# Second-layer output weights prepared while the input half runs, parked in DRAM and read back

## The chip, the core and the metric

The kernel runs on one core of a Trainium2 chip: TensorE (PE in the profile) for matmuls, VectorE (DVE), ScalarE (ACT), GpSimd (POOL), and SyncE (SP), which here only issues DMA transfers. Each engine works through its own queue in order. The metric is device time in microseconds, the median of several runs.

## The reference

Local plus downsampled attention gives x of 2304 tokens by 512. Two feed-forward layers follow, in float32:

```python
h = x @ w_in;  g = where(h > 0, h, exp(min(h, 0)) - 1);  x = g @ w_out        # first layer
h = x @ w2_in; r = maximum(h, 0); g = s * (r * r) + b;   out = g @ w2_out     # second layer
```

w_in and w2_in are 512 x 2048, w_out and w2_out are 2048 x 512. The weights come as float64, so they have to be turned into float32 on the core before use.

## The kernel before

**Two halves of the second layer.** The w2_in half (h and g of all tokens) has its first product at 542.3 us, among the last ones of the first layer, and its last at 742 us; the w2_out half follows. The stretch in which the weight tiles pass from one to the other is called the exchange here. A float32 product is made of three passes: each operand is split into a rounded part (hi) and the remainder (lo), and hi x hi, lo x hi and hi x lo are added in PSUM.

**Seven products instead of eight.** Tokens are taken as five groups: four groups of two 256-token blocks and one single block (group 3). For a pair of blocks, 2 x 2 blocks are multiplied with seven products (numbers 1 to 7, in the order ROW for w2_in and COL for w2_out) of sums and differences of half-matrices. So each weight pair p (eight pairs, 256 of the 2048 columns each) needs two tiles: the values (wb) and four half-matrix sums (wa), both as hi and lo.

**Making a weight pair**, `halves(kind, p, due)` (L1238): one load of 1 MB of float64 into a `raw` tile; Prelu on ACT (L1256), a shift (L1258) and a combine (L1260) on DVE, which give float32 values; four sums of 256 columns on DVE (L1277); then a hi copy on ACT and a lo remainder on DVE or POOL for the values (L1279, L1281) and for the sums (L1283, L1284). kind 0 is w2_in, kind 1 is w2_out. hi and lo of w2_out go to the same 16 SBUF tiles that hold w2_in's, so they can be written only when the last group has used those.

**Units and quads.** `unit` (L1382) makes seven products of twelve 256-column matmuls for two pairs (four units a group), DVE adds the PSUM banks into h tiles (`total`, L1432), ACT applies Relu (L1442), Square (L1370) and the affine step (L1376), and SP stores the tile to DRAM as `gd` (L1443). `quad` (L1456) loads four g tiles (`gb`, L1469), makes sums of them on DVE (L1496 to L1502), splits each of seven operands into an F tile (ACT L1478, DVE or POOL L1479) and runs one half, 24 matmuls on four pairs, per operand. Two quads make a group.

**Places.** SBUF outside the weights is an arena: `ar.place` (L46) gives a tag n tiles at an offset of a ground, with a phase. A place can be used once all places of earlier phases under it are through. The nine `st` places hold h tiles, seven `X` the split inputs, three `F` the split g operands, `raw1` one raw w2_out tile, `cv` five converted pairs, `St` two sets of sums.

**What sets the order.** The code describes operations with a due time. `Plan.emit` (L147) then lays them out with a price for each, always taking the soonest or the most urgent, and writes each engine's queue in that order; the waits between engines follow from the data. `MM` is the price of one 256-column matmul, `GBS` that of a byte of DMA, which `slow` multiplies. Where the plan sees PE idle, `fill` (L132) calls `keep_warm` (L1542), which puts matmuls on a zero tile `wz` into PE's queue (L1548): their number is fixed when the program is built.

## Time and profile before

| | |
|---|---|
| median of 3 runs | 942.58 us (939.83 to 944.01) |
| profiled execution | 943.77 us |
| its span, first to last instruction | 942.0 us |
| PE busy | 931.9 us, 99% |
| DVE, ACT, POOL busy | 701.4, 556.8, 398.3 us |
| mean granted TensorE clock | 0.989 |
| moved by DMA | 126.1 MB, 134 GB/s on average |

Busy time counts the zero-tile matmuls of L1548 as PE work, so PE's share alone doesn't tell how much of it is products. For a wait, the engine's own timeline and the chain of work that ended last are to be read together: the chain says which engine's work the end hung on in each stretch. Starts in a timeline are exact; a duration of matmuls that follow each other overlaps the next one, so the time of a run is the distance between starts.

### The profile page before, as it was taken

How to read it: one execution, taken by the hardware profiler on the slowest of the kernel's cores; microseconds unless marked ns; L12 is line 12 of the kernel's file. 1: busy time of each engine (PE TensorE's matmuls, PEld its weight loads, DVE VectorE, ACT ScalarE, POOL GpSimd, SP SyncE). 2: the span in 40 equal slices, each digit the busy share in tenths (PEclk: the TensorE clock that was granted, in tenths of full speed). 3: DMA queues.
4: the chain of work that ended last, by engine and by line, in shares of the span. 5: the costliest groups of instructions: out<-in, count | busy, mean ns of one | idle time of the engine just before them, and what ended most of it. 6: DMA issues, size and time to landing. Idle time of an engine off the chain costs nothing. (4 is left out here: it accounts for less than half of the span.)

```text
span 942.0 us, 21568 instructions
## 1 busy us (share of the span) xinstructions
PE 931.9 (99%) x8577; PEld 882.9 (94%) x8577; DVE 701.4 (74%) x1087; ACT 556.8 (59%) x1207; POOL 398.3 (42%) x356
## 2 busy tenths in 40 slices
PE   8999999999999999999999999999999999999998
PEld 4879999999999999999999999999999679999998
DVE  5467768888887889888716688777549988786875
ACT  5488766564554545444656678887978734334332
POOL 4567657797887778776456742000001100000000
PEclk9599999999999999999999999999999999999999
DMA  9739776545442425334112255636545353343511
GB/s 192 192 120 233 201 183 164 142 135 116 111 129 69 132 60 146 97 101 119 62 44 92 88 183 190 192 131 215 174 130 168 118 183 125 102 157 116 167 36 42
DMA packets 118917, 126.11 MB, mean 134 GB/s; under 512 B 50464, under 2 KB 93472, under 8 KB 118816
## 3 DMA queue, kind: packets, MB, share of 16 engines
q1 hardware_dynamic: 117024, 124.29, 46.1%
q8 instruction: 67, 1.10, 0.5%
q10 hardware_dynamic: 1792, 0.44, 0.2%
q14 instruction: 34, 0.28, 0.1%
HBM read 92.73 MB, written 31.98 MB: 132 GB/s over the span
## 5 line engine op out<-in xcount | busy, mean ns | idle before, releaser
L1034 PE MATMUL acc<-split,w 128*128 128x256 f32 x1728 | 234.6, 285 | 0.0
L1034 PEld LDWEIGHTS acc<-split,w 128*128 128x128 f32 x1728 | 216.4, 188 | 2.9 <-issue 1.9
L988 PE MATMUL h<-split,w 128*128 128x256 f32 x1488 | 204.9, 286 | 0.9 <-DVE work L1012 0.7
L988 PEld LDWEIGHTS h<-split,w 128*128 128x128 f32 x1488 | 188.6, 190 | 3.7 <-DVE work L1012 1.3
L413 POOL TENSOR_TENSOR split<-work,split 128x256 fp32r<-128x256 f32 (+2 forms) x156 | 141.9, 917 | 92.6 <-ACT split L405 80.9
L1487 PE MATMUL acc<-w,attn 128*128 128x256 f32 x864 | 106.2, 281 | 0.0
L405 ACT ACTIVATE split<-work 128x256 fp32r<-128x256 f32 (+2 forms) x162 | 66.5, 423 | 64.5 <-PE acc L1034 30.9
L1487 PEld LDWEIGHTS acc<-w,attn 128*128 128x128 f32 x864 | 104.1, 189 | 0.0
L1012 DVE SCALAR_TENSOR_TENSOR work<-work,h 128x256 f32<-128x256 f32 x124 | 50.5, 414 | 67.5 <-ACT work L1010 67.1
L1422 PE MATMUL acc<-attn,w 128*128 128x256 f32 x768 | 99.7, 282 | 0.0
L1422 PEld LDWEIGHTS acc<-attn,w 128*128 128x128 f32 x768 | 95.3, 188 | 0.0
L1008 ACT ACTIVATE work<-h 128x256 f32<-128x256 f32 x124 | 47.1, 380 | 75.9 <-PE h L988 49.7
L1478 ACT ACTIVATE attn<-work 128x1024 fp32r<-128x1024 f32 x35 | 37.2, 1062 | 64.6 <-DVE work L1502 22.7
L1479 POOL TENSOR_TENSOR attn<-split,attn 128x1024 fp32r<-128x1024 f32 x2 | 5.4, 2682 | 158.4 <-PE at L1422 155.5
L413 POOL TENSOR_TENSOR work<-work 128x896 f32<-128x896 f32 (+1 forms) x41 | 68.2, 1672 | 5.9 <-DVE work L930 5.4
L930 DVE TENSOR_REDUCE work<-work 128x128 f32<-128x896 f32 x36 | 63.5, 1788 | 4.8 <-POOL work L413 4.8
L1010 ACT ACTIVATE work<-work 128x256 f32<-128x256 f32 x144 | 60.0, 416 | 3.9
L1376 ACT ACTIVATE split<-split,sb 128x512 f32<-128x512 f32 x62 | 48.6, 808 | 12.0 <-DVE split L1373 11.2
L1487 PE MATMUL h<-w,attn 128*128 128x256 f32 x432 | 54.6, 281 | 0.7 <-DVE attn L1479 0.7
L1487 PEld LDWEIGHTS h<-w,attn 128*128 128x128 f32 x432 | 52.5, 189 | 1.0 <-DVE attn L1479 0.9
L1479 DVE TENSOR_TENSOR attn<-work,attn 128x1024 fp32r<-128x1024 f32 x35 | 42.4, 1221 | 12.8 <-ACT attn L1478 12.5
L1422 PE MATMUL h<-attn,w 128*128 128x256 f32 x384 | 51.4, 282 | 0.0
(194 smaller groups left out, 1651.6 us busy)
## 6 DMA issues: line engine op xcount, KB each, us to landing
gd<-split SPq DMA_DIRECT2D x57, 256.0 KB
split<-gd SPq DMA_DIRECT2D x28, 512.0 KB
work<-in_moe_w_in_dram SPq DMA_DIRECT2D x16, 512.0 KB
work<-in_moe_w_out_dram SPq DMA_DIRECT2D x16, 512.0 KB
work<-in_moe_w_in_dram SPq DMA_DIRECT2D x8, 1024.0 KB
work<-in_moe_w_out_dram SPq DMA_DIRECT2D x8, 1024.0 KB
work<-in_k_dram SPq DMA_DIRECT2D x17, 320.0 KB
work<-in_v_dram SPq DMA_DIRECT2D x17, 320.0 KB
```

The costliest lines, as they stand in the source:

```text
L405: a = (0.11 + n / 1200, lambda: nc.scalar.activation(out=out(), in_=src(), func=ACTF.Copy, scale=scale))
L413: f = lambda e: lambda: e.tensor_tensor(out=out(), in0=in0(), in1=in1(), op=alu)
L930: op("dve", 0.07 + 14 * D / 546, lambda: nc.vector.tensor_reduce(out=vo()[:, WD + j * D:WD + (j + 2) * D].rearrange("p (j d) -> p j d", j= ...
L988: nc.tensor.matmul(ps(), lhsT=w()[:, wpart, 0, c * 128:(c + 1) * 128], rhs=x.at(xpart)[:, c, :], start=first and i == 0, stop=last and i = ...
L1008: op("act", ta + 0.07, lambda: nc.scalar.activation(out=e(), in_=ps(), func=ACTF.Relu, scale=-1.0), r=[ps], w=[r1], u=[e], due=due)
L1010: op("act", ta, lambda: nc.scalar.activation(out=e(), in_=e(), func=ACTF.Exp, scale=-1.0), r=[r1], w=[r2], u=[e], due=due)
L1012: op("dve", td, lambda: nc.vector.scalar_tensor_tensor(out=e(), in0=e(), scalar=-1.0, in1=ps(), op0=ALU.add, op1=ALU.max), r=[r2, ps], w=[ ...
L1034: nc.tensor.matmul(acc()[:, c * N:(c + 1) * N], lhsT=wo[:, cc * 128:(cc + 1) * 128], rhs=g(), start=first and c == 0, stop=end and c == 1)
L1376: [lambda: nc.scalar.activation(out=h(), in_=h(), func=ACTF.Identity, scale=sb2[:, 0:1], bias=sb2[:, 1:2]), lambda: nc.vector.tensor_scala ...
L1422: nc.tensor.matmul(ps[:, q * 256:(q + 1) * 256], lhsT=factor(0, w[2 * u + q], i, wi, c), rhs=x[i]()[:, xi].rearrange("p (c t) -> p c t", c ...
L1479: on(lambda e: e.tensor_tensor(out=f()[:, 1], in0=src(), in1=f()[:, 0].bitcast(F32), op=ALU.subtract), 1024, ("dve", "pool"), r=[*r, hi], ...
L1487: nc.tensor.matmul(m[i]()[:, c * 256:(c + 1) * 256], lhsT=f()[:, xi, o:o + 128], rhs=factor(1, w[pair], i, wi, 0), start=qd == 0 and p == ...
```

## The change

`halves` is split up. `weights` loads and converts a pair and makes its sums. For w2_in, `halves` then splits them into hi and lo as before. For w2_out, `ahead` runs `weights` for all eight pairs while the w2_in half is on, from the second group on by its due times, twelve us apart, and stores the float32 values (`wb`) and the sums (`wa`) to DRAM, 512 KB each. At the exchange `kept_halves` loads them back into `cv` tiles and only makes hi (ACT) and lo (DVE).

Places change with it: w2_out's raw tiles use the two `raw` places, the converted values get three `cw` places, the first four g tiles lie where `raw` was and need not wait for h tiles, `sq` moves to the ground `split`, and `cv` has four places.

Numbers of the plan change too: a matmul is priced 0.1185 us instead of 0.1085, the second layer's large transfers at 0.85 of the byte price, x2d loads are due 11 us earlier, and the seven products of a unit run in the order 1, 2, 6, 7, 5, 4, 3.

```diff
     RAW, EV, R_, WU = 0, 16384, 24576, 26624
+    ar.place("cw", 1, 4096, "work", 0, 1, EV)
+    ar.place("cw", 2, 4096, "work", 0, 2, WU + 4096)
     ar.place("X", 7, 4096, "attn", 1, 1)
...
     ar.place("st", 1, 2048, "work", 0, 1, R_)
-    ar.place("raw1", 1, 8192, "work", 0, 1, RAW)
-    ar.place("cv", 1, 4096, "work", 0, 2, EV)
-    ar.place("cv", 2, 4096, "work", 0, 2, WU + 4096)
-    ar.place("cv", 2, 4096, "work", 0, 2, RAW + 8192)
+    ar.place("cv", 2, 4096, "work", 0, 3, EV)
+    ar.place("cv", 2, 4096, "work", 0, 3, WU + 4096)
     ar.place("F", 3, 8192, "attn", 1, 3, 0)
-    ar.place("gb", 6, 4096, "split", 1, 3, 0)
-    ar.place("gb", 2, 4096, "work", 0, 3, EV)
-    ar.place("sq", 2, 4096, "work", 0, 3, RAW)
-    ar.place("o", 1, 2048, "work", 0, 3, R_)
-    ar.place("o", 4, 2048, "work", 0, 3, RAW + 8192)
-    ar.place("o", 4, 2048, "work", 0, 3, WU + 4096)
+    ar.place("gb", 4, 4096, "work", 0, 2, RAW)
+    ar.place("gb", 4, 4096, "split", 1, 3, 0)
+    ar.place("sq", 2, 4096, "split", 1, 3, 16384)
+    ar.place("o", 1, 2048, "work", 0, 4, R_)
+    ar.place("o", 4, 2048, "work", 0, 4, EV)
+    ar.place("o", 4, 2048, "work", 0, 4, WU + 4096)
     ps_t = pool("ps_t", 2, space=PSUM)
...
-    MM = 0.1085
-    ROW = (1, 2, 5, 6, 7, 4, 3)
+    MM = 0.1185
+    SL = 0.85
+    ROW = (1, 2, 6, 7, 5, 4, 3)
     COL = (2, 1, 5, 6, 7, 3, 4)
...
-    def halves(kind, p, due):
-        wa, wb = Buf(wp, f"w{2 * p}", [128, 2, 4, 256], F32R), Buf(wp, f"w{2 * p + 1}", [128, 2, 2 * DM], F32R)
-        wa.part, wb.part = parts(), parts()
-        raw = Buf(ar, "raw1" if kind else "raw", [128, 2 * DM, 2], I32)
-        cv = Buf(ar, "cv", [128, 2 * DM], I32) if kind else raw
+    def weights(kind, p, due, early):
+        raw = Buf(ar, "raw", [128, 2 * DM, 2], I32)
+        cv = Buf(ar, "cw", [128, 2 * DM], I32) if kind else raw
         got, u, shifted, made = (Buf(None, x, None) for x in ("got", "u", "shifted", "made"))
...
-        load(got, 1048576, ld, due - 20 - 80 * kind, u=[raw])
+        load(got, 1048576, ld, early - 8, u=[raw], slow=SL)
         act(lambda: nc.scalar.activation(out=high().bitcast(F32), in_=high().bitcast(F32), func=ACTF.Prelu,
-                                         scale=2.0 ** -112, alpha=-2.0 ** 32), 2 * DM, r=[got], w=[u], u=[raw], due=due - 60 * kind)
+                                         scale=2.0 ** -112, alpha=-2.0 ** 32), 2 * DM, r=[got], w=[u], u=[raw], due=early)
         op("dve", 0.07 + DM / 960, lambda: nc.vector.tensor_scalar(
-            out=low(), in0=low(), scalar1=29, scalar2=None, op0=ALU.logical_shift_right), r=[got], w=[shifted], u=[raw], due=due - 60 * kind, lock=True)
+            out=low(), in0=low(), scalar1=29, scalar2=None, op0=ALU.logical_shift_right), r=[got], w=[shifted], u=[raw], due=early, lock=True)
         op("dve", 0.07 + 2.5 * DM / 960, lambda: nc.vector.scalar_tensor_tensor(
             out=cv() if kind else low(), in0=high(), scalar=3, in1=low(), op0=ALU.logical_shift_left, op1=ALU.bitwise_or),
-            r=[u, shifted], w=[made], u=[raw, cv], due=due - 60 * kind, lock=True)
+            r=[u, shifted], w=[made], u=[raw, cv], due=early, lock=True)
         src = (lambda: cv().bitcast(F32)) if kind else (lambda: raw()[:, :, 0].bitcast(F32))
...
                r=[made, *(sums[i] for i in need)], w=[sums[k]], u=[cv, st], due=due)
-        act(lambda: nc.scalar.activation(out=wb()[:, 0], in_=src(), func=ACTF.Copy), 2 * DM,
-            r=[made], w=[wb.part[0]], u=[cv, wb], due=due)
-        on(lambda e: e.tensor_tensor(out=wb()[:, 1], in0=src(), in1=wb()[:, 0].bitcast(F32), op=ALU.subtract), 2 * DM, (("pool", "dve") if kind == 0 else ("dve",)),
-           r=[made, wb.part[0]], w=[wb.part[1]], u=[cv, wb], due=due)
-        act(lambda: nc.scalar.activation(out=wa()[:, 0], in_=st(), func=ACTF.Copy), 1024, r=sums, w=[wa.part[0]], u=[st, wa], due=due)
-        on(lambda e: e.tensor_tensor(out=wa()[:, 1], in0=st(), in1=wa()[:, 0].bitcast(F32), op=ALU.subtract), 1024, (("pool", "dve") if kind == 0 else ("dve",)),
-           r=[*sums, wa.part[0]], w=[wa.part[1]], u=[st, wa], due=due)
+        return cv, src, [made], st, sums
+    def hi_lo(t, parts, src, r, u, due, n=1024, lo=("dve",)):
+        act(lambda: nc.scalar.activation(out=t()[:, 0], in_=src(), func=ACTF.Copy), n, r=r, w=[parts[0]], u=[t, *u], due=due)
+        on(lambda e: e.tensor_tensor(out=t()[:, 1], in0=src(), in1=t()[:, 0].bitcast(F32), op=ALU.subtract), n, lo,
+           r=[*r, parts[0]], w=[parts[1]], u=[t, *u], due=due)
+    def slots(p):
+        wa, wb = (Buf(wp, f"w{2 * p + i}", [128, 2, 1024], F32R) for i in range(2))
+        wa.part, wb.part = parts(), parts()
         return wa, wb
+    def halves(p, due):
+        wa, wb = slots(p)
+        cv, src, r, st, sums = weights(0, p, due, due)
+        hi_lo(wb, wb.part, src, r, [cv], due, lo=("pool", "dve"))
+        hi_lo(wa, wa.part, lambda: st().rearrange("p k n -> p (k n)"), sums, [st], due, lo=("pool", "dve"))
+        return wa, wb
+    kept_w = {}
+    def ahead(p, due):
+        cv, src, r, st, sums = weights(1, p, due, due)
+        kept_w[p] = dram_buf(f"wa{p}", [128, 1024]), dram_buf(f"wb{p}", [128, 2 * DM])
+        load(kept_w[p][1], 524288, lambda: nc.sync.dma_start(out=kept_w[p][1].t.bitcast(I32), in_=cv()), due, r=r, u=[cv], slow=SL)
+        load(kept_w[p][0], 524288, lambda: nc.sync.dma_start(out=kept_w[p][0].t, in_=st().rearrange("p k n -> p (k n)")), due,
+             r=sums, u=[st], slow=SL)
+    def kept_halves(p, due):
+        w = slots(p)
+        for i in (1, 0):
+            cv, got = Buf(ar, "cv", [128, 1024]), Buf(None, "got", None)
+            load(got, 524288, lambda cv=cv, src=kept_w[p][i]: nc.sync.dma_start(out=cv(), in_=src.t), due - 10, r=[kept_w[p][i]], u=[cv], slow=SL)
+            hi_lo(w[i], w[i].part, cv, [got], [cv], due)
+        return w
...
         if i in MADE or i == (4 if kind else 3):
-            x = wa()[:, part, MADE.get(i, 3)]
+            x = wa()[:, part].rearrange("p (k n) -> p k n", k=4)[:, MADE.get(i, 3)]
             return x if kind else x[:, c * 128:(c + 1) * 128]
...
             out=b().rearrange("p (c t) -> p c t", c=2),
-            in_=x2d[j].t[k * 256:(k + 1) * 256, :].rearrange("(c p) t -> p c t", p=128)), due - 14, r=[x2d[j]], u=[b])
+            in_=x2d[j].t[k * 256:(k + 1) * 256, :].rearrange("(c p) t -> p c t", p=128)), due - 25, r=[x2d[j]], u=[b])
         return b, got
...
         for dst, fn, n in stores:
-            load(dst, n, fn, due, r=[g], u=[h])
+            load(dst, n, fn, due, r=[g], u=[h], slow=SL)
...
             load(got[blk], 524288, lambda b=a[blk], src=src: nc.sync.dma_start(out=b(), in_=src.t.rearrange("p a t -> p (a t)")),
-                 d - 12, r=[src], u=[a[blk]])
+                 d - 12, r=[src], u=[a[blk]], slow=SL)
         sq = Buf(ar, "sq", [128, 1024])
...
-    w2 = [halves(0, p, time2[0, 0, p // 2] - 12) for p in range(PAIRS)]
+    w2 = [halves(p, time2[0, 0, p // 2] - 12) for p in range(PAIRS)]
+    for p in range(PAIRS):
+        ahead(p, time2[0, 1, 0] + 12 * p)
     for gi in range(len(groups)):
...
             unit(gi, u, xs, w2)
-    w2 = [halves(1, p, time2[1, 0, p // 4] - 12) for p in range(PAIRS)]
+    w2 = [kept_halves(p, time2[1, 0, p // 4] - 12) for p in range(PAIRS)]
     for gi in order2:
```

Two places show what moves. The first is DVE's queue at the exchange, from the end of the last unit on. `w8` to `w15` are the tiles of pairs 4 to 7, `work` holds raw, converted and summed weights and g sums. Before:

```order
L1277 TENSOR_TENSOR work_155<-work_155 128x256 x8
L1281 TENSOR_TENSOR w9_9533<-work_155,w9_9533 128x1024
L1284 TENSOR_TENSOR w8_9745<-work_155,w8_9745 128x1024
L1281 TENSOR_TENSOR w11_9537<-work_155,w11_9537 128x1024
L1277 TENSOR_TENSOR work_155<-work_155 128x256 x4
L1284 TENSOR_TENSOR w10_9747<-work_155,w10_9747 128x1024
L1281 TENSOR_TENSOR w13_9751<-work_155,w13_9751 128x1024
L1277 TENSOR_TENSOR work_155<-work_155 128x256 x4
L1284 TENSOR_TENSOR w12_9764<-work_155,w12_9764 128x1024
L1281 TENSOR_TENSOR w15_9756<-work_155,w15_9756 128x1024
L1284 TENSOR_TENSOR w14_9775<-work_155,w14_9775 128x1024
L1496 TENSOR_TENSOR work_155<-split_7420 128x1024
```

Now (L1463 is a total, L1510 the remainder of an F tile, L1283 that of a weight tile, L1529 and L1533 are g sums):

```order
L1510 TENSOR_TENSOR attn_6364<-work_171,attn_6364 128x1024
L1463 TENSOR_TENSOR split_7439<-h_9699,split_7439 128x512
L1283 TENSOR_TENSOR w9_9680<-work_171,w9_9680 128x1024
L1283 TENSOR_TENSOR w8_9713<-work_171,w8_9713 128x1024
L1510 TENSOR_TENSOR attn_6364<-split_7439,attn_6364 128x1024
L1529 TENSOR_TENSOR split_7439<-split_7439,work_171 128x1024
L1283 TENSOR_TENSOR w11_9783<-work_171,w11_9783 128x1024
L1283 TENSOR_TENSOR w10_9788<-work_171,w10_9788 128x1024
L1510 TENSOR_TENSOR attn_6364<-split_7439,attn_6364 128x1024
L1283 TENSOR_TENSOR w13_9820<-work_171,w13_9820 128x1024
L1510 TENSOR_TENSOR attn_6364<-work_171,attn_6364 128x1024
```

The sums of 256 columns (16 in the rows before, counting the factors) are gone from here, and g sums and F remainders stand between the weight remainders instead of behind all of them.

The second is SP's queue over the end of the last unit, where `gd4` are stores of the last group's h tiles and `gd0` are g tiles of the first. Before:

```order
L1443 DMA gd4_1_0_148<-split_7420 128x512
L1443 DMA gd4_1_3_149<-split_7420 128x512
L1443 DMA gd4_1_1_150<-split_7420 128x512
L1443 DMA gd4_1_2_151<-split_7420 128x512
L1469 DMA split_7420<-gd0_0_2_119 128x1024
L1469 DMA split_7420<-gd0_0_3_117 128x1024
L1469 DMA split_7420<-gd0_1_1_122 128x1024
L1469 DMA split_7420<-gd0_1_0_120 128x1024
L1469 DMA work_155<-gd0_1_2_123 128x1024
L1469 DMA work_155<-gd0_1_3_121 128x1024
```

Now (L1315 loads a parked weight tile, L1474 stores an h tile, L1500 loads a g tile):

```order
L1474 DMA gd4_1_0_164<-split_7439 128x512
L1500 DMA split_7439<-gd0_1_1_138 128x1024
L1315 DMA work_171<-wb6_129 128x1024
L1500 DMA split_7439<-gd0_1_0_136 128x1024
L1474 DMA gd4_1_3_165<-split_7439 128x512
L1315 DMA work_171<-wa6_128 128x1024
L1474 DMA gd4_1_1_166<-work_171 128x512
L1474 DMA gd4_1_2_167<-split_7439 128x512
L1500 DMA work_171<-gd0_1_2_139 128x1024
L1315 DMA work_171<-wb7_131 128x1024
L1315 DMA work_171<-wa7_130 128x1024
L1500 DMA split_7439<-gd0_1_3_137 128x1024
```

Before, all but two of the first group's eight g tiles stood behind the last group's stores. Now the loads of the last two pairs stand among those stores and the second quad's g tiles; the first quad's four g tiles stand some 60 rows further up, among the stores of the third group.

PE's queue in the second layer has 125 zero-tile matmuls of 512 columns and 19 of 128 before, and 17 and 10 now. The other instructions of PE are the same in number.

## Rows read from the trace of the kernel before

**Rows 1.** Windows: us, busy PE PEld DVE ACT POOL (instructions), PEclk, DMA share, GB/s

```profile
560.00:730.00 170.00, 170.00 (x1411) 168.11 (x1410) 122.63 (x186) 140.08 (x213) 10.18 (x4) 1.00 0.52 169
730.00:767.70 37.70, 36.86 (x220) 23.39 (x220) 34.13 (x46) 23.00 (x30) 2.87 (x1) 1.00 0.43 145
```

**Rows 2.** Timeline of PE at the exchange: start, us, line, operation, [idle before, releaser]

```profile
729.09 1.60 PE L1422 MATMUL h<-attn,w 128*128 128x256 f32 x12
730.53 3.15 PE L1548 MATMUL at<-wz 128*128 128x512 bf16 x16
...
742.46 20.52 PE L1548 MATMUL at<-wz 128*128 128x512 bf16 x95
762.78 0.47 PE L1487 MATMUL h<-w,attn 128*128 128x256 f32 x2
763.95 2.85 PE L1487 MATMUL h<-w,attn 128*128 128x256 f32 x22 [0.69 <-DVE attn L1479]
```

**Rows 3.** Line L1548, 560 to 780 us: ns min/median/max, first and last start, forms

```profile
L1548 PE MATMUL at<-wz x144: 219/379/390, 585.5 to 773.5; 128*128 128x512 bf16 x125, 128*128 128x128 bf16 x19
```

**Rows 4.** The chain that ended last, in order of time: start us, us, what

```profile
736.95 0.61 DVE split L1432
...
740.06 2.12 ACT split L1376 x3
...
744.22 1.03 ACT split L1442 x2
...
748.41 0.95 ACT w L1283
...
749.39 1.23 DVE w L1284
750.61 1.14 DVE w L1281
751.75 0.34 DVE work L1277
...
752.12 1.10 DVE work L1277 x3
...
760.35 1.15 DVE work L1496
...
763.95 2.85 PE h L1487 x22
...
796.54 2.85 PE acc L1487 x24
```

**Rows 5.** Windows, columns as in rows 1, for the DMA share and rate

```profile
604.00:608.00 4.00, 4.00 (x35) 4.00 (x35) 3.55 (x7) 2.47 (x5) 0.00 (x0) 1.00 1.00 379
748.00:752.00 4.00, 4.00 (x21) 1.80 (x19) 2.61 (x3) 4.00 (x5) 0.00 (x0) 1.00 1.05 314
...
759.50:760.00 0.50, 0.50 (x4) 0.24 (x3) 0.50 (x1) 0.00 (x0) 0.00 (x0) 1.00 0.00 0
760.00:764.00 4.00, 3.31 (x18) 1.56 (x16) 3.93 (x5) 1.06 (x1) 0.00 (x0) 1.00 0.79 251
...
764.50:765.00 0.50, 0.50 (x7) 0.50 (x6) 0.50 (x1) 0.00 (x0) 0.00 (x0) 1.00 0.00 0
```

**Rows 6.** Timeline of SP's DMA queue at the exchange: start us, us, line, transfer

```profile
748.86 2.43 SPq L1469 DMA_DIRECT2D split<-gd  x4
759.29 1.41 SPq L1469 DMA_DIRECT2D work<-gd  x2
```

**Rows 7.** Windows near the start, columns as in rows 1, for the granted clock

```profile
20.00:30.00 10.00, 8.85 (x149) 7.16 (x148) 4.81 (x16) 6.09 (x28) 7.26 (x10) 0.73 1.08 276
30.00:40.00 10.00, 10.00 (x106) 7.72 (x106) 5.02 (x8) 5.89 (x13) 4.88 (x5) 0.50 0.62 116
40.00:50.00 10.00, 10.00 (x62) 7.94 (x60) 3.92 (x8) 4.02 (x9) 4.12 (x5) 0.75 0.64 211
```

**Rows 8.** Waits of SP's queue: line, releaser, us in total, times, longest us

```profile
SPq L1443 <- ACT split L1376: 79.5, 40, 16.7
```

## Prediction

> **What bounds the kernel now.** I began with the busy time of each engine by stretch [rows 1]. TensorE (PE) counts as busy everywhere, 170.00 us of 170 while the w2_in half runs and 36.86 of 37.7 at the exchange. That is not all work. PE's timeline at the exchange [rows 2] shows runs of L1548, matmuls on a tile of zeros that only keep the engine running: 3.15 us at 730.53 and 20.52 us at 742.46, then 0.69 us of plain waiting for DVE. So PE had no product from 742.46 to 763.95. These fillers are instructions, placed where the plan foresaw an idle PE, and they take their time whether or not the wait is still there. In the second FFN there are 125 of 512 columns and 19 of 128 [rows 3].
>
> Next, what PE really waited for. The chain that ended last [rows 4] does not pass through PE before 763.95. It runs from a DVE total at 736.95 through a row of ACT steps on the last h tiles (Relu, Square, affine) to a weight copy on ACT at 748.41, then through DVE: remainders of the w2_out weights (L1281, L1284, 1.13 to 1.23 us each) and half-matrix sums (L1277, four per pair, about 1.45 us in all), one pair after the other, until the first g sum (L1496, 760.35). DVE's queue is in order, so the g sum that the third half of the first quad needs stood behind all the weights. DVE is busy 34.13 of these 37.7 us [rows 1]. The bound is therefore PE everywhere but in this stretch, where it is DVE's queue with an ACT lead-in.
>
> **The change part by part.** *Fillers.* PE's order counts 125 and 19 fillers in this part before, and 17 and 10 now: one and three in group 1, two and three in group 2's first unit, five and one, then two and two, at group 2's end, seven and one after the third half of the first quad. The long run gives the price: 742.46 to 762.78 is 20.32 us for 95, so 0.214 us each [rows 2]; a 128-column one I take at a quarter, 0.056 us, an estimate. Before: 125 x 0.214 + 19 x 0.056 = 27.8 us. After: 17 x 0.214 + 10 x 0.056 = 4.2 us. **Minus 23.6 us**, all on PE's own queue and so on the path. The plain wait of 0.69 us belonged to the old queue: **minus 0.7**. All products stay, at 1.44 us for twelve matmuls (729.09 to 730.53) and 2.85 us for a half [rows 2, 4].
>
> *DVE and ACT work.* The number of conversions, sums, copies and remainders is the same as before on both engines, apart from two F remainders that leave POOL for DVE and two affine steps that come to ACT. What moves is the place. The 32 sums, about 8 x 1.45 = 11.6 us of DVE, and what was left of the conversions, go from the exchange into the w2_in half, where DVE was busy 122.63 of 170 us [rows 1]; that idle time hides them. At the exchange DVE keeps 16 remainders. Does it fit? From the last group's first total to the F remainder of the fourth half (the one behind the last filler run) DVE's order has 28 totals and 4 squarings at 0.61 us and 18 operations on 1024 columns at 1.14 us [rows 4]: 19.5 + 20.5 = 40.0 us. PE spends 28 x 1.44 + 3 x 2.85 + 1.6 = 50.5 us over the same part. So DVE has 10 us in hand.
>
> ACT is tighter. Over the last group's four units its order has 4 bank copies, 12 Relu, 13 Square, 17 affine and 12 copies of 1024 columns; at 0.71 us for an affine step, 0.95 for 1024 columns and Relu's 0.52 for the rest [rows 4] that is 38.5 us, and four more copies before the fourth half make 42.3, against 50.5. From the second unit on ACT is full, since the four weight copies of a unit fall on top of its 6.5 us of own work: 10.3 us for PE's 10.1. And the plan counts an affine step at 0.1 + 512/1200 = 0.53 us, as any ACT operation of that width, where the trace has 0.71 (2.12 for three [rows 4]): 17 x 0.18 = 3.1 us that the plan does not see. **Plus 0 to 3.1 us; I take 1.5,** because the filler run there already pays for part of it and DVE has slack.
>
> *DMA.* Added are 16 stores and 16 loads of 512 KB, 16.8 MB. At the 314 to 379 GB/s of the fullest windows [rows 5] they are 44 to 53 us of transfer. The DMA engines were busy 0.52 of the half and 0.43 of the exchange, about 105 us [rows 1]; 150 to 158 us in the 183 that are left of this stretch is a share near 0.85. So they fit on average, and the question is order. At the exchange the loads of pair 6 wait for places that DVE frees about 2 us after the last product, and go out with two g tiles and a store, 2.4 MB: 6 to 8 us at those rates, plus 0.7 us from issue to first byte (759.29 to 760.0 [rows 5, 6]), so they are there 9 to 11 us after the last product. ACT asks for them at 7 to 9 us, PE for their products at 20. The wait is up to 4 us of ACT's and is mostly covered. The Trainium skill, DMA: Bandwidth & Descriptors, section Anatomy of one DMA, gives about 2 us fixed plus the bytes over 436 GB/s, so an estimate of 3.2 us for one such tile, and holds the cost against many small round trips through HBM; the trace agrees in size, two tiles issued from 759.29 on having moved by 764.5. By that rule all 32 transfers one after the other would be 102 us, and only their overlap makes them free.
>
> *SP's queue and the places.* A store of a pair's sums or values waits on SP for DVE, and what is queued behind it are stores of h tiles and x2d loads; the nine places for h tiles, at eight tiles a unit, give about one unit of room, 10 us. The x2d loads are due 11 us earlier, and the first quad's g tiles go where w2_out's raw tiles were, so they are loaded before the exchange, not at 748.86 as now [rows 6]. The changed row order and pace move no work. The w2_in half had no PE wait besides fillers [rows 1]; with DVE and ACT 11 us fuller and the plan's pace now the true one, there is less slack. **Plus 0 to 5 us; I take 1.0,** near the zero of today's row.
>
> Sum against the profiled execution (943.77 us, span 942.0): 943.77 - 23.6 - 0.7 + 1.5 + 1.0 = 922.0. It lies 1.2 us above the median of the runs shown, 942.58, so **920.8 us** for a median.
>
> **The rivals.** *A, late weights:* the loads of pairs 6 and 7 leave behind g tiles and behind h stores that wait for ACT; if two of them come a landing (about 4 us) later than ACT asks, ACT's queue holds the F copies too, and PE waits unfilled: 8 us, **929**. For it: ACT full in the last three units. Against: 20 us until PE needs these pairs.
>
> *B, the wait stays:* if the third half still cannot start, for a reason other than DVE's queue (g tiles from 748.86 [rows 6] or F places under the X tiles), the change does not do what it says, and PE idles 18 to 20 us where the fillers were: 918.3 + 19 = **937 to 939**. Against: in DVE's new order the g sums precede most of the weights.
>
> *C, the clock:* between 20 and 50 us the granted clock was 0.73, 0.50 and 0.75 of full [rows 7], that is at or on the way to 1.2 GHz; this costs 2.7 + 5.0 + 2.5 = 10.2 us of full-speed work. An unfilled wait of some us at the exchange could bring the same: **931**. Against: 0.69 us of idle PE there left the clock at 1.00 [rows 1, 2]. The Trainium skill, TensorE: Matmul & The Clock Gate, Part 1, says that an idle TensorE falls back to half its clock; by it fewer fillers speak against this change, and rows 7 agree that the fall exists. It adds this case, nothing to the sum.
>
> *D, slower:* there are two places for half-matrix sums, so the sums of pair p, in DVE's queue ahead of h totals, wait until the store of pair p-2 has landed. SP issues in order, and its stores of h tiles wait for ACT 40 times, 79.5 us in all, 16.7 at the longest [rows 8]. Should such a wait plus a landing (16.7 + 4.1) outrun the 12 us between pairs at four of six pairs, DVE stands 4 x 8.8 = 35 us and PE's banks with it: 918.3 + 35 = **953**. It decides from a mean of about 5 us per pair. Against: 79.5/40 is 2.0 us.
>
> **How the numbers follow.** The forecast (917 to 925) has 0.76, A 0.13, C 0.04, B 0.04, D 0.03. The lower end of the range is the sum with both unknowns at zero, 918.3, less about 1 for the scatter of runs: 917. The upper end takes in A, and both unknowns at their upper bounds (918.3 + 8.1 = 926.4): 930. That leaves B, C and D out, about 0.11. A measurement of this kernel can tell about 0.5%, 4.7 us, from no change: faster by more than that 0.93 (forecast, A, C), within it 0.04 (B), slower 0.03 (D).
>
> **What would show it.** Right: filler rows in the second FFN near 27 and 4 us in all; the last w2_in product and the first halves of a quad back to back; weight stores spread over the half; no sums at the exchange. Affine steps at 0.71 us with ACT busy nearly without a break in the last three units would show the 1.5 us term. Wrong would be: PE waits of several us on ACT or DVE behind the third half (A, B), a granted clock under 1.00 after the exchange (C), DVE idle for a DMA ahead of its sums (D), or PE waits of more than 5 us in the w2_in half, by which my smallest term would be the mis-sized one.

## The result, and the profile after

The changed kernel took **929.15 us** (median of four runs, 927.33 to 930.24) against 941.21 for the kernel before on the same chip (median of four): 0.987 of it, 95% interval 0.984 to 0.990. The forecast was 920.8 us with a range of 917 to 930. The direction and the range held; the likeliest value was 8.3 us too low. The forecast's own band, 917 to 925 with a chance of 0.76, does not hold the measured time. The range reached it only because its upper end took in rival A; the sum with both of its terms at their upper bounds is 926.4. The profiled execution took 927.33 us, with a span of 925.6. Two single executions, 1721 us of the kernel of e9 below and 1472 us of the kernel before beside it, lie far from all others and are in no ratio or median here.

The windows of the changed kernel, with columns as in [rows 1] (the second FFN is the second layer):

```profile
30.00:60.00 30.00, 29.66 (x337) 23.65 (x336) 15.01 (x34) 18.86 (x57) 15.67 (x17) 0.78 0.51 142
560.00:730.00 170.00, 166.31 (x1370) 163.71 (x1369) 129.60 (x202) 139.63 (x214) 8.86 (x4) 1.00 0.75 252
744.00:746.00 2.00, 0.90 (x5) 0.70 (x6) 1.65 (x2) 2.00 (x3) 0.00 (x0) 1.00 0.95 322
746.00:748.00 2.00, 2.00 (x12) 2.00 (x12) 2.00 (x3) 1.28 (x3) 0.00 (x0) 0.53 0.98 321
748.00:750.00 2.00, 2.00 (x12) 1.91 (x12) 2.00 (x2) 2.00 (x3) 0.00 (x0) 0.61 1.06 393
```

In the w2_in half the DMA share rose from 0.52 [rows 1] to 0.75 and DVE from 122.6 to 129.6 us. The direction was foreseen, the size was not: the prediction has DVE and ACT 11 us fuller, and ACT's 139.6 us are no more than the 140.1 before [rows 1]. And PE is no longer busy for all 170 us: 3.7 us are plain waits. At the exchange the granted clock is 0.53 and 0.61 of full for 4 us, close to the lower of its two levels (1.2 of 2.4 GHz), where it was 1.00 before. The fillers, by shape, from the second FFN's start to the end (line, instructions, names, count, busy us, mean ns):

```profile
L1581 PE MATMUL at<-wz 128*128 128x512 bf16 x14 | 3.5, 381 | 0.0
L1581 PE MATMUL acc<-wz 128*128 128x512 bf16 x3 | 1.0, 386 | 0.0
L1581 PE MATMUL at<-wz 128*128 128x128 bf16 x4 | 0.7, 219 | 0.0
L1581 PE MATMUL acc<-wz 128*128 128x128 bf16 x6 | 0.7, 219 | 0.0
```

These are the 17 and 10 of the prediction; [rows 3] had 125 and 19. What PE waited for without a filler in the same stretch (us in total, times, longest):

```profile
PE at L1453 <- DVE split L1463: 2.5, 1, 2.5
PE h L1518 <- ACT attn L1509: 2.4, 1, 2.4
PE h L1518 <- DVE attn L1510: 0.8, 1, 0.8
PE acc L1425 <- ACT split L1479: 0.5, 1, 0.5
PE acc L1518 <- DVE attn L1510: 0.4, 1, 0.4
PE acc L1453 <- ACT attn L1352: 0.4, 1, 0.4
PE acc L1453 <- DVE attn L1353: 0.2, 1, 0.2
```

That is 7.2 us, at two main places. The first is the exchange. PE's timeline there, which answers to [rows 2]:

```profile
739.08 2.87 PE L1518 MATMUL acc<-w,attn 128*128 128x256 f32 x22 [0.44 <-DVE attn L1510]
744.34 0.50 PE L1518 MATMUL h<-w,attn 128*128 128x256 f32 x2 [2.38 <-ACT attn L1509]
745.60 4.41 PE L1518 MATMUL h<-w,attn 128*128 128x256 f32 x22 [0.76 <-DVE attn L1510]
749.85 1.74 PE L1581 MATMUL at<-wz 128*128 128x512 bf16 x8
```

The third half now follows the second after 2.4 and 0.8 us of waiting, not after 20 us of fillers. But its last 22 matmuls took 4.41 us, where the same 22 took 2.85 us at full clock [rows 2]: 1.6 us more. What it waited for is the last line of ACT's timeline:

```profile
735.05 0.82 ACT L1407 ACTIVATE split<-split,sb 128x512 f32<-128x512 f32 x1
735.78 1.05 ACT L1282 ACTIVATE w<-work 128x1024 fp32r<-128x1024 f32 x1
...
740.51 0.80 ACT L1407 ACTIVATE work<-work,sb 128x512 f32<-128x512 f32 x1
741.22 0.62 ACT L1473 ACTIVATE split<-split 128x512 f32<-128x512 f32 x1
741.87 0.63 ACT L1401 ACTIVATE split<-split 128x512 f32<-128x512 f32 x1
742.53 0.81 ACT L1407 ACTIVATE split<-split,sb 128x512 f32<-128x512 f32 x1
743.25 1.04 ACT L1509 ACTIVATE attn<-split 128x1024 fp32r<-128x1024 f32 x1
```

ACT had no gap of more than 0.1 us from 717 to 746 us: Relu (L1473), Square (L1401) and affine (L1407) of the last h tiles, weight copies (L1282), and only at 743.25 the F copy (L1509). An affine step takes 0.71 us from start to start (741.22 less 740.51), and the plan counts 0.53.

The second place is the start of the third group, one timeline of ACT and one of DVE:

```profile
631.81 1.51 ACT L1407 ACTIVATE split<-split,sb 128x512 f32<-128x512 f32 x2
633.22 0.57 ACT L1479 ACTIVATE split<-acc 128x512 f32<-128x512 f32 x1
```

```profile
631.00 1.55 DVE L1276 TENSOR_TENSOR work<-work 128x256 f32<-128x256 f32 x4
632.47 0.69 DVE L1257 TENSOR_SCALAR work<-work 128x1024 int32<-128x1024 int32 x1
633.83 0.69 DVE L1463 TENSOR_TENSOR split<-at,split 128x512 f32<-128x512 f32 x1 [0.67 <-ACT split L1479]
```

The product at 634.58 needs a bank that the total at 633.83 sets free; the total needs ACT's bank copy (L1479), which stood behind two affine steps. The moved sums (L1276) and the shift (L1257) lie ahead of it on DVE, but they ended 0.67 us before it could start. ACT was not full here: at 628.71 it had just waited 1.96 us for an earlier total of DVE (L1463), and its row of steps began late.

**A yardstick for the runs.** The first 545 us are the same work in every kernel here, yet they end at different times. The granted clock between 30 and 60 us was 0.78 above, 0.75 in the kernel before, 0.72 in one run below and 0.97 in another, and the second FFN's first product on an "at" bank started at 544.4, 546.6, 546.8 and 540.1 us. So beside the ratio I give the second FFN alone: the profile's span less that start. From it I take the fillers (by their number in the order, 0.214 and 0.056 us each), the waits listed for PE, and what a lower clock cost (matmuls there against the same at full clock: 4.41 against 2.85 us for 22). If this accounting is right, the rest is the same everywhere.

| kernel | ratio to before, 95% | second FFN, us | fillers | waits | clock | rest |
|---|---|---|---|---|---|---|
| before | 1 | 395.4 | 27.8 | 0.7 | 0 | 366.9 |
| changed | 0.987 (0.984 to 0.990) | 381.2 | 4.2 | 7.2 | 1.6 | 368.2 |
| e1 numbers alone | 0.996 (0.994 to 0.999) | 392.2 | 24.2 | 1.3 | 0 | 366.7 |
| e2 parking alone | 1.001 (0.998 to 1.003) | 397.5 | 26.7 | 3.3 | 0 | 367.5 |
| e3 g places back | 0.992 (0.989 to 0.994) | 388.2 | 10.3 | 6.1 | 2.8 | 369.0 |
| e4 third half kept warm | 0.983 (0.980 to 0.987) | 380.0 | 7.6 | 4.1 | 0 | 368.3 |
| e5 four affine steps on DVE | 0.986 (0.982 to 0.991) | 381.9 | 6.7 | 6.3 | 0 | 368.9 |
| e6 e5, no fillers at the exchange | 0.985 (0.982 to 0.989) | 380.9 | 2.6 | 9.3 | 0 | 369.0 |
| e7 no fillers | 0.987 (0.983 to 0.991) | 382.4 | 0 | 11.8 | 2.6 | 368.0 |
| e8 true affine price | 0.984 (0.979 to 0.988) | 381.7 | 12.2 | 2.4 | 1.5 | 365.6 |
| e9 true price, affine steps on DVE | 0.982 (0.980 to 0.984) | 374.3 | 4.8 | 2.9 | 0 | 366.6 |
| e10 changed, again | 0.987 (0.985 to 0.989) | 381.2 | 4.2 | 7.2 | 1.5 | 368.3 |

The rest lies between 365.6 and 369.0 while the second FFN goes from 374 to 398. So fillers, unfilled waits and clock account for these differences to within about 2 us of the middle. Part of what is left may be a tail of each wait. The profile counts a wait from the modelled end of the matmul before it; twelve matmuls last 1.60 us by themselves and take 1.44 us where others follow [rows 2]. By these two numbers a wait costs an estimated 0.16 us more than is listed, and the changed kernel has seven waits where there was one.

### The profile page after: what moved, and what is told of

It reads as the page before. It is cut to its first block, busy times and chain, and to the rows that moved or that the text cites. A ratio compares the mean times of both kernels' runs of the same rounds, so it can differ in the third digit from the quotient of the medians.

```text
span 925.6 us, 21389 instructions
## 1 busy us (share of the span) xinstructions
PE 910.1 (98%) x8460; PEld 872.6 (94%) x8460; DVE 700.8 (76%) x1089; ACT 556.7 (60%) x1208; POOL 392.0 (42%) x353
## 5 line engine op out<-in xcount | busy, mean ns | idle before, releaser
L413 POOL TENSOR_TENSOR split<-work,split 128x256 fp32r<-128x256 f32 (+2 forms) x154 | 137.0, 897 | 88.8 <-ACT split L405 72.8
L1509 ACT ACTIVATE attn<-split 128x1024 fp32r<-128x1024 f32 x43 | 45.5, 1060 | 74.5 <-PE acc L1518 29.8
L1510 DVE TENSOR_TENSOR attn<-split,attn 128x1024 fp32r<-128x1024 f32 x43 | 52.4, 1221 | 19.9 <-ACT attn L1509 19.6
L1407 ACT ACTIVATE split<-split,sb 128x512 f32<-128x512 f32 x64 | 50.7, 809 | 5.6 <-DVE split L1404 4.8
L1283 POOL TENSOR_TENSOR w<-work,w 128x1024 fp32r<-128x1024 f32 x16 | 40.5, 2540 | 20.9 <-ACT w L1282 20.9
```

The costliest lines, as they stand in the source:

```text
L413: f = lambda e: lambda: e.tensor_tensor(out=out(), in0=in0(), in1=in1(), op=alu)
L1407: [lambda: nc.scalar.activation(out=h(), in_=h(), func=ACTF.Identity, scale=sb2[:, 0:1], bias=sb2[:, 1:2]), lambda: nc.vector.tensor_scala ...
L1510: on(lambda e: e.tensor_tensor(out=f()[:, 1], in0=src(), in1=f()[:, 0].bitcast(F32), op=ALU.subtract), 1024, ("dve", "pool"), r=[*r, hi], ...
```

## The experiments

**Which part brings the gain?** First the numbers without the DRAM tiles, on the kernel before:

```
-    MM = 0.1085
-    ROW = (1, 2, 5, 6, 7, 4, 3)
+    MM = 0.1185
+    SL = 0.85
+    ROW = (1, 2, 6, 7, 5, 4, 3)
```

(and `slow=SL` on the h stores and g loads, x2d loads due at 25 us ahead for 14).

> The kernel before with only the change's numbers: product price 0.1185, the new row order, transfers counted at 0.85 of their time, x2d loads 11 us earlier. No values or sums go to DRAM, and no tile changes its place. TensorE's order has 112 fillers of 512 columns and 4 of 128 in the second FFN (125 and 19 before, 17 and 10 after). Theory 'together' (neither part does anything alone, the fillers in the order are the time): 112 x 0.214 + 4 x 0.056 = 24.2 us against 27.8, so 941.2 - 3.6 = 937.6 us, 935 to 941. Rival 'pace' (the truer pace by itself removes the waits): 932 or less, with products where the fillers were. The DVE queue at the exchange should still show 32 sums.

Measured 938.70 us (before 942.45), 0.996, as "together" had it. The fillers stand where they stood: one run of 100, from 739.39 us on, where the kernel before has its 95 from 742.46 on [rows 2]. All of the "at" bank:

```profile
L1549 PE MATMUL at<-wz 128*128 128x512 bf16 x110 | 24.4, 379 | 0.0
```

Then the opposite, the DRAM tiles and new places with the old numbers:

```
-    MM = 0.1185
-    SL = 0.85
-    ROW = (1, 2, 6, 7, 5, 4, 3)
+    MM = 0.1085
+    SL = 1.0
+    ROW = (1, 2, 5, 6, 7, 4, 3)
```

> The changed kernel with the old numbers: product price 0.1085, old row order, transfers at full time, x2d loads as late as before. Values and sums still go through DRAM and the tiles keep their new places. TensorE's order has 102 fillers of 512 columns and 20 of 128 there, which are 22.9 us. The changed kernel's profile without its fillers, waits and slow clock is 927.3 - 4.2 - 3.7 - 3.6 - 1.8 = 914.0. Theory 'together': the fillers are time on the path and cover most true waits: 914 + 23 = 937 for a profile, 936 to 942 as a median, so no more than 0.5% under the kernel before. Rival 'parking' (moving the conversions and sums out of the exchange is the whole gain): 930 to 933.

Measured 942.61 us, 1.001: no gain at all. The order has in fact 117 and 29 fillers, 24 more than the expectation counts. With 26.7 us of them and these waits on top of the 914.0 us of the expectation the sum comes to 944.0 us, and the profiled run took 943.63:

```profile
PE acc L1453 <- DVE split L1463: 1.2, 1, 1.2
PE h L1518 <- DVE attn L1510: 1.2, 1, 1.2
PE h L1453 <- DVE split L1463: 0.9, 1, 0.9
```

So "together" holds: alone the numbers give 3.7 us and the DRAM tiles nothing, both give 12. With the old numbers PE's order has fillers at twenty places (the longest run is 36, within the half); with the new numbers and the sums still at the exchange it has the one run of 100. The four numbers were changed as one: whether it is the product price that does it, or the row order, the byte price or the earlier x2d loads, is not shown.

**Do the g tiles need their free places?**

```
-    ar.place("gb", 4, 4096, "work", 0, 2, RAW)
-    ar.place("gb", 4, 4096, "split", 1, 3, 0)
-    ar.place("sq", 2, 4096, "split", 1, 3, 16384)
+    ar.place("gb", 6, 4096, "split", 1, 3, 0)
+    ar.place("sq", 2, 4096, "work", 0, 2, RAW)
```

> The changed kernel, but the g tiles have no places at the old raw tiles: six places behind the h places, the two sum tiles at the raw tiles. TensorE's order has 46 fillers of 512 and 9 of 128 columns (17 and 10 in the changed kernel), 36 of them between the second and the third half of the first quad. That is 6.2 us more of fillers, at the place where the changed kernel waits 3.6 us and loses 1.8 us to a lower clock. Theory 'ACT' (ACT is what the third half waits for): the fillers cover that wait, 929.2 + 6.2 - 5.4 = 930, 928 to 933. Rival 'places' (the g tiles' loads are late without the free places, and the change needs them): PE waits behind the fillers too, 935 or more, with g loads as last releaser.

Measured 933.59 us, 0.992, nearer to "places" than to "ACT". The extra fillers did not cover the wait. PE's timeline, and one link of the chain that ended last:

```profile
742.69 8.05 PE L1580 MATMUL at<-wz 128*128 128x512 bf16 x38
752.67 0.50 PE L1517 MATMUL h<-w,attn 128*128 128x256 f32 x2 [1.92 <-ACT attn L1508]
753.92 5.06 PE L1517 MATMUL h<-w,attn 128*128 128x256 f32 x22 [0.76 <-DVE attn L1509]
```

```profile
743.54 6.71 DMA gd<-split
750.25 1.23 DVE work L1526
```

In the chain, as the profile infers it, an h store, 6.7 us from issue to landing, stands right ahead of the first g sum. ACT then waited 2.5 us for that sum. So the third half was late for a DMA here, and for ACT's queue in the changed kernel. The wait of the same 1.9 and 0.8 us, this time right behind 8 us of fillers, again lowered the clock:

```profile
754.00:756.00 2.00, 2.00 (x9) 2.00 (x10) 2.00 (x2) 1.28 (x2) 0.00 (x0) 0.50 0.51 207
756.00:758.00 2.00, 2.00 (x11) 2.00 (x11) 2.00 (x3) 2.00 (x3) 0.00 (x0) 0.50 0.90 293
```

**Is the clock's fall a consequence of the wait?** Sixteen matmuls on zeros in the third half's own bank, ahead of its first product, which overwrites them:

```
+                if gi == 0 and qd == 0 and i == 5:
+                    for _ in range(16):
+                        nc.tensor.matmul(m[i](), lhsT=wz, rhs=..., start=True, stop=True)
                 for p, pair in enumerate(pairs):
```

> The changed kernel with 16 matmuls on the tile of zeros, 512 columns, written into the third half's own bank ahead of its first product (which overwrites them), so that TensorE works while it waits for ACT's copy: 3.4 us at full clock, in place of 2.4 us of wait and a little more. Theory 'clock' (the fall to 0.53 and 0.61 of full between 746 and 750 us came from the unfilled wait, and costs 1.8 us): granted clock 1.00 there, the third half in 2.6 us where it was 4.4, 927.4 us, 926.5 to 928.5. Rival 'lateness only' (the half is fed by ACT and DVE at that pace, the clock costs nothing by itself): 929 to 930.

Measured 926.71 us, 0.983. PE's timeline and a window:

```profile
742.74 3.63 PE L1516 MATMUL h<-wz 128*128 128x512 bf16 x16
746.01 3.43 PE L1521 MATMUL h<-w,attn 128*128 128x256 f32 x24
```

```profile
746.00:748.00 2.00, 2.00 (x16) 1.80 (x15) 1.97 (x3) 1.28 (x3) 0.00 (x0) 1.00 0.95 302
```

The clock stays at 1.00, and the half's 24 matmuls take 3.4 us, where in the changed kernel they began at 744.34 and ended at 750.0. The second FFN is 1.2 us shorter in the profiles (381.2 to 380.0). Against the changed kernel the two intervals overlap, so the ratio alone would not show it. In this profile the filled wait kept the clock up; e7 below shows that an unfilled one does not always lower it.

**Is ACT what the third half waits for?** The four affine steps of the last unit of the w2_in half go to DVE:

```
-        op(["act", "dve"], [0.1 + 512 / 1200, 0.07 + 512 / 1920], ...
+        forms = [("act", 0.1 + 512 / 1200, ...), ("dve", 0.07 + 512 / 1920, ...)]
+        forms = forms[1:] if due > time2[0, 4, 2] + 10 else forms[:1]
+        op(*(list(z) for z in zip(*forms)), ...
```

> The changed kernel with the four affine steps of the last two-group unit's h tiles given to DVE in place of ACT (all others stay on ACT). That takes 4 x 0.71 = 2.8 us out of the row of ACT steps that ran without a break from 717 to 744 us, behind which the third half's copy stood. The plan sets 27 fillers of 512 and 17 of 128 columns (17 and 10 in the changed kernel), 2.5 us more, now behind the third half and later. Theory 'ACT': the third half waits under 1 us where it waited 3.1, and the clock stays 1.00, so 929.2 - 2.3 - 1.8 + 2.5 = 927.6, 926 to 929. Rival 'loads' (the weight loads, 5.2 us from issue to landing, set ACT's pace): the half is as late as before, part of the wait is only moved, 930 to 932.

Measured 927.50 us, 0.986, with PE at the exchange:

```profile
737.67 2.85 PE L1518 MATMUL acc<-w,attn 128*128 128x256 f32 x22 [1.08 <-POOL attn L1510]
740.84 0.51 PE L1518 MATMUL h<-w,attn 128*128 128x256 f32 x2 [0.31 <-ACT attn L1509]
742.10 2.85 PE L1518 MATMUL h<-w,attn 128*128 128x256 f32 x22 [0.75 <-DVE attn L1510]
```

The third half waits 1.1 us where it waited 3.1, at full clock: "ACT" holds for its place. The time did not follow. A remainder that the plan now gave to POOL (1.1 us), a later DVE wait (0.6) and 2.5 us more of fillers took the gain back: 381.9 us against 381.2. The same order without the fillers at the exchange (`if t0 > 700: return` ahead of the plan's filling):

> As the run before, and no fillers from the first quad on (10 of 512 and 7 of 128 columns are left, all in the w2_in half). Theory 'ACT' with covered or no waits: 927.6 - 4.1 of fillers there = 923.5, 922 to 925. Rival 'clock' (there are true waits of ACT and DVE behind the third half, now unfilled, and the clock falls after them): 927 to 930, with a granted clock of 0.5 to 0.6 in some windows between 740 and 765 us.

Measured 927.66 us, 0.985. Of the 4.1 us of fillers taken out, 3.0 came back as waits (6.3 to 9.3 us in all), each of those at the exchange 1.5 us or less, and the clock stayed at 1.00 in every window. The rival's time, then, without its mechanism. Without any filler in the second FFN, on the changed kernel (`if t0 > 530: return`):

> The changed kernel without any filler in the second FFN (17 of 512 and 10 of 128 columns before, 4.2 us), the order of everything else unchanged. If fillers are plain cost: 929.2 - 4.2 = 925.0. If they stand where PE would wait in any case (5 of them right ahead of the 2.55 us wait at the third group's start): 928 to 929.5, with that wait near 3.3 us and the one behind the third half near 1.5 us. If the longer unfilled waits also lower the clock at a second place: 931 or more.

Measured 929.00 us, 0.987: no change, though 4.2 us of instructions are gone. The waits rose by 4.6 us. The clock now fell at the third group's start:

```profile
630.25 2.93 PE L1455 MATMUL at<-attn,w 128*128 128x256 f32 x12 [3.15 <-DVE split L1465]
```

```profile
632.00:634.00 2.00, 2.00 (x11) 2.00 (x11) 1.13 (x1) 2.00 (x3) 0.00 (x0) 0.50 0.69 187
```

At the exchange it did not fall, although PE waited there unfilled as long as in the changed kernel:

```profile
742.70 0.51 PE L1520 MATMUL h<-w,attn 128*128 128x256 f32 x2 [2.41 <-ACT attn L1511]
743.95 2.88 PE L1520 MATMUL h<-w,attn 128*128 128x256 f32 x22 [0.75 <-DVE attn L1512]
```

The 22 matmuls took 2.88 us, and the granted clock is 1.00 in every window from 736 to 752 us. So the same wait at the same place can lower the clock or leave it; what decides is not shown.

On the whole the fillers left in the changed kernel are no cost to be saved: nearly each stands where PE would wait.

**Does the plan's wrong price matter?** One number:

```
-        op(["act", "dve"], [0.1 + 512 / 1200, 0.07 + 512 / 1920],
+        op(["act", "dve"], [0.28 + 512 / 1200, 0.07 + 512 / 1920],
```

> The changed kernel with one number of the plan changed: an affine step on ACT counts 0.28 + 512/1200 = 0.71 us, as in the trace, where it counted 0.53. No work changes; order and fillers do: 54 fillers of 512 and 12 of 128 columns, 12.2 us (4.2 in the changed kernel), 9 us of them at the exchange. Theory 'ACT': the plan now sees ACT's real load, PE's unfilled waits in the second FFN (7.2 us) nearly vanish and the clock stays 1.00; 929.2 - 7.2 - 1.8 + 8.0 = 928.2, 927 to 931: same as the changed kernel, since the plan foresees the waits but does not remove them. Rival 'better order' (with the true price the plan puts the third half's copy ahead): 925 or less. Rival 'fillers on top': 934 or more, with the waits still there.

Measured 925.56 us, 0.984, between "ACT" and "better order". Its four runs lie at 923.3, 923.4, 927.8 and 929.0, and its interval contains the changed kernel's ratio, so this run does not show it to be faster. In the profiles the second FFN is as long (381.7 to 381.2). PE's unfilled waits fell from 7.2 to 2.4 us, none of them in the half, and the fillers rose by 8. Foreseeing the waits does not remove them. Here the rest is 1 to 3 us under the others, for which I have no cause. Last, the true price with affine steps on DVE where the plan likes, in the fifth group and in the last three units of the second, ahead of the third group's start:

```
+        forms = [("act", 0.28 + 512 / 1200, ...), ("dve", 0.07 + 512 / 1920, ...)]
+        forms = forms[::-1] if due > time2[0, 4, 0] or time2[0, 1, 2] < due < time2[0, 2, 1] else forms[:1]
```

> The changed kernel with the true price of an affine step in the plan (0.71 us, as in the run with the price alone) and eleven affine steps on DVE in place of ACT: those of the last two-group units and of the units around the third group's start. The plan sets 21 fillers of 512 and 5 of 128 columns (54 and 12 with the price alone), none of them at the third group's start but two. Theory 'ACT': the two places where the changed kernel waits for ACT (2.6 us at the third group's start, 3.1 us at the third half) are relieved, not only foreseen: PE's unfilled waits under 3 us in all where they were 7.2, clock 1.00 throughout, 929.2 - 4.2 - 1.8 + 0.6 = 923.8, 921.5 to 926; so 2 us under the run with the price alone. Rival 'DVE next' (DVE, busy 0.9 there, takes the steps at 0.7 us too and its sums come late): PE waits on DVE of 4 us or more, 927 to 931.

Measured 922.50 us (median of five runs, 920.29 to 925.35), 0.982 of before, against 928.24 us and 0.987 for the changed kernel in the same series; the intervals (0.980 to 0.984, 0.985 to 0.989) do not meet. The second FFN is 6.9 us shorter, 5.3 of it in the table's columns of fillers, waits and clock. This is what "ACT" had foreseen. Of PE's waits two are left, together under 3 us, and the clock is 1.00 in every window from 545 to 780 us:

```profile
PE acc L1518 <- POOL attn L1510: 1.9, 1, 1.9
PE acc L1518 <- DVE attn L1510: 1.0, 1, 1.0
```

The affine steps did not cost DVE what they cost ACT (split tiles, over the whole second FFN, both forms):

```profile
L1407 DVE TENSOR_SCALAR split<-split,sb 128x512 f32<-128x512 f32 x24 | 14.7, 629 | 0.7 <-ACT split L1401 0.5
```

```profile
L1406 ACT ACTIVATE split<-split,sb 128x512 f32<-128x512 f32 x39 | 30.6, 807 | 0.4
```

That is 24 of the 27 steps that went to DVE. The expectation has eleven, so this run moved more work than it says. This version beats both kernels. The changed kernel itself was run once more beside it:

> The changed kernel itself, beside the others on one chip: 0.985 to 0.988 of the kernel before, about 929. Its waits should stand where the first profile had them (2.6 us at the third group's start, 2.4 and 0.8 us ahead of the third half). If the fall of the clock behind the third half's wait is a matter of chance and not of the wait, this profile will not show it, or at another place.

The waits stand where they stood, and the clock falls at the same place, in both profiles of this kernel:

```profile
746.00:748.00 2.00, 1.59 (x7) 1.59 (x8) 1.97 (x3) 1.28 (x3) 0.00 (x0) 0.63 0.94 301
748.00:750.00 2.00, 2.00 (x12) 2.00 (x11) 2.00 (x3) 2.00 (x3) 0.00 (x0) 0.52 1.03 397
```

## Why the prediction was right in direction and 8 us too low

*Fillers, minus 23.6: right.* Their number and price held, and the accounting above rests on the same price in twelve profiles. (One reading was loose: PE's first two products behind the long run stand at 762.78 [rows 2], not at 763.95.)

*The plain wait, minus 0.7: wrong in kind.* The old 0.69 us is gone, but the same third half waits at the same place for the next engine.

*ACT at the exchange, 0 to 3.1, taken 1.5: mis-sized.* It measured 3.6 us of waits and 1.6 us of clock, 5.2 in all, above its own upper end. I had named the right queue and the wrong price (0.71 against 0.53). The step that failed is "the filler run there already pays for part of it". I had compared totals, 42.3 us of ACT work against 50.5 of PE, and that run stands behind the third half. The F copy was late at one place, ahead of the run; e5 shows it by taking 2.8 us from ACT ahead of that copy. The bound was also drawn from the price alone, without what a wait does to the clock. I had that as rival C, worth 10 us or nothing; it came as 1.6 us in the forecast's own case.

*The w2_in half, 0 to 5, taken 1.0: 3.7.* Inside its bounds, near the wrong end. I took the value near the zero of [rows 1] because DVE and ACT had idle time over the 170 us. At the third group's start that sum says nothing: there ACT's affine steps, the moved sums and shifts and the group's input differences meet within 4 us. With affine steps moved to DVE the idle time does suffice: e9 has no wait in the half and three fillers. The true price alone only fills the waits: e8 has none in the half, but 22 fillers.

*Places, loads, stores.* Free places for g tiles were worth more than I had said: without them an h store's landing is on the chain (e3). Rival D (DVE standing for the stores of sums) did not come: the 40 sums in the second FFN had 0.5 us of idle DVE ahead of them in all. Rival B did not come either. Rival A had the measured time, 929, but not its mechanism: at the exchange ACT's queue did hold the F copy, but ACT itself waited for a load for 0.1 us at most from 717 to 746 us. One load of a pair's values is on the chain, 5.24 us from its issue at 718.98 to 724.23, where rival A had a landing at about 4 us; ACT had other steps to do meanwhile. The Trainium skill, DMA: Bandwidth & Descriptors, section Anatomy of one DMA, had given me an estimate of 3.2 us for such a tile; that section describes transfers that GpSimd issues, and these are SP's. With others in flight the trace has 5.24, and the measurement decides. So it is in part luck that the range, stretched to 930 for A, held the time. Of the prediction's own signs of being wrong one came, a granted clock under 1.00 (C). Waits of PE on ACT and DVE came too, but ahead of the third half and in it, not behind it.

*Profile and median.* The sum stood 1.2 us above the median of before. The profiled run of the changed kernel was 1.8 us under its own median, 3.0 us the other way, mostly offset by 2.2 us that the profile won ahead of the second FFN. From 922.0 the terms give: half +2.7, exchange +3.7, start -2.2, which is 926.2; the profile had 927.33, and 1.1 us is left (six waits more than before at the 0.16 us estimated above would be 1.0; no run tests it). With 1.2 and 1.8 us from profile to median this makes the 8.3 us.

## What to carry to other kernels

A filler counts as a saving only if nothing else is late at its place: take it out of the order, and read what PE would wait for next, engine by engine, at that very instruction. Compare the order of the in-order queues there and not their totals. Where a plan sets the order, a price that is a quarter too low (0.53 for 0.71 us), on an engine that is full at one place, hides its waits. Here the true price alone turned waits into fillers (e8), and the time of the second FFN fell only when more work went to another engine as well (e9); four steps moved at the old price (e5) did not do it.

## What the runs showed of the chip

A few us of waiting can cost more than themselves. 2.4 and 0.8 us of idle PE with two matmuls between brought 0.53 and 0.61 of the granted clock for 4 us; 1.6 and 0.8 us did the same in e8 (22 matmuls in 4.39 us). But 2.4 and 0.8 us at the same place in e7 left it at 1.00. 1.9 and 1.0 us with a half between them (e9) and a single 2.5 us at the third group's start did not, while 3.15 us there, behind a shorter wait, gave 0.50 (e7). Fillers right ahead of the wait did not protect (e3); with fillers in it the clock stayed at 1.00 (e4). So these rows give no rule for when a wait lowers the clock. The Trainium skill, TensorE: Matmul & The Clock Gate, Part 1, says that an idle TensorE falls back to half its clock; the windows at 0.50 agree that it happens, and e7 shows that a wait of 2.4 and 0.8 us need not do it.

The same first 545 us differed by 6.7 us between profiles, with the granted clock of 30 to 60 us from 0.97 to 0.72:

```profile
30.00:60.00 30.00, 29.62 (x267) 22.58 (x265) 15.85 (x32) 18.05 (x51) 14.23 (x15) 0.75 0.54 145
```

That is the kernel before, with PE busy 29.62 of 30 us; what sets the clock there was not tried. These 6.7 us are as large as the effects of half of these experiments, so a stretch of the profile tells more than the ratio.
